# Eight stores of half-size sums from GpSimd's queue to the sync engine's, with new engine orders (one core, attention and a gated MLP)

## The chip, the cores and the metric

The kernel runs on one core of a Trainium2 chip. The metric is device time in microseconds (us). TensorE (PE) does the matmuls, VectorE (DVE) elementwise work, ScalarE (ACT) copies and activations. GpSimd (POOL) and the sync engine (SP) issue transfers here and compute next to nothing. Transfers run on 16 DMA engines, whichever engine issues them.

## The reference

Inputs are bfloat16. `x` is 2048 tokens by 1024; the MLP is 3584 wide; attention has 32 heads of 32, each token looking at 8 earlier tokens at a distance of 0, 2, ..., 14.

```python
xn = layernorm(x)
q, k, v = split(xn @ wqkv)                     # 32 heads of 32
logits = einsum("bhsd,bhswd->bhsw", q, kg) * scale     # kg: k at positions s - 2w, w = 0..7
attn = softmax(where(mask, logits, -1e9))
s = einsum("bhsw,bhswd->bhsd", attn, vg) @ wo
h = silu(xn @ w1) * (xn @ w3)
g = silu(h @ w2)
return x + s * g
```

## The kernel before

The 2048 tokens are two halves (`b` = 0, 1) of 1024, each made of two chunks of 512 (`c` = 0 to 3). For a half the order of work is: layer norm and a transposition of x, the q, k and v products, the up and gate products in 14 steps of 256 columns (`up_step`), the down product (`mlp_down`), and the output projection (`wo`). Attention runs on DVE beside these matmuls. Every matrix product is done in the Strassen-Winograd way: seven products of quarter blocks in place of eight, with sums and differences of blocks made by DVE beforehand and added up by ACT and DVE afterwards. So DVE has much to do for the matmuls too.

Many of the sums are of weights, the same for both halves of the tokens. In the first half they are stored to DRAM and in the second half they are loaded back.

`mlp_down(b)` contracts over 3584 in two halves, `fh`. It takes seven products, each 4 groups (128 tokens each, `g`) of 14 matmuls, with operands of plain down weights (`w2`, loaded in two parts `q` of 896 KB) or of sums of them (`t2`, loaded from `t_dram`). Two of the seven are split once more the same way (`product2`): these are called `l1` (plain weights) and `l2` (a sum). Each needs four half-size sums of its weights, made by DVE in the first half: `l1t1` to `l1t4`, `l2t1` to `l2t4`. Each is 448 KB, and a `dma` call stores it to `lt_dram` (`put_l10` to `put_l13` and `put_l20` to `put_l23`; the last digit is the sum's number less one). In the second half `get_l..` loads them. Beside the weights' sums there are sums of the left operand, `l1s1` to `l1s4` and `l2s1` to `l2s4`, also by DVE. The buffer of `l2t1` and of `l2s1` is the one in which x of the next chunk lay; `l2t1` therefore waits until that x is transposed into `xT` (four transposing transfers, `turn2_0` to `turn2_3`, issued by ACT, after the normalisations `nrm2_0` to `nrm2_3`). The first part of the last plain down weights is loaded into that buffer in turn; the second part into one that is free earlier. The four transpositions of the chunk after it (`turn3_0` to `turn3_3`) are issued by SP.

The order of the work is not left to a scheduler of the compiler. `Plan` records every operation with a cost, a simulation of the five engines' queues makes an order for each engine (`simulate`), and `ORDER`, five lists of moves, one for each engine, changes these orders: `(a, b)` takes operation `a` out and puts it behind `b`. Each engine runs its list in order and waits where an operand is not ready. For a transfer the cost is a size in KB times a factor by name (`COST`) over a rate (`plan.rate`). These costs only decide the order; they change no transfer.

A transfer is issued by the engine that `dma` is given:

```python
def dma(eng, name, o, a, rd, wr, kb, late=0.0):
    e = {SP: nc.sync, POOL: nc.gpsimd, ACT: nc.scalar}[eng]
```

All matmuls of plain tiles are recorded by the helper at line 582, those of the split products at 1542 (down) and 1271 (up); DVE's sums at 591, ACT's copies at 596, transfers at 623, transpositions at 784 and 792. So in the profile a line is a helper's, and an operation is told by its tile and its time. In the profile's tile names, `r` is any of the six weight buffers, `ltl_dram` is `lt_dram`, `a` holds attention's products, `E` the softmax weights, `xs` sums of x or of the left operand, `mm` the PSUM banks and `k` the buffers that hold copies of PSUM.

Of the kernel before, what the change touches and what calls it, by code (L numbers as in the profile page):

```python
# [14 lines left out]
PE, DVE, ACT, POOL, SP = range(5)  # L15
# [27 lines left out]
class Plan:  # L43
# [409 lines left out]
def kernel(  # L453
# [27 lines left out]
    NQ = 7  # L481
# [49 lines left out]
    plan = Plan()  # L531
# [891 lines left out]
    def mlp_down(b):  # L1423
# [71 lines left out]
        def product2(ps, w, bdt, xa, xc, ya, yc, sa, sc, rows, tdst, names, marks=(None, None), mixed=False):  # L1495
# [9 lines left out]
            def tsum(q, fn, x, y, rd):  # L1505
# [3 lines left out]
                if names in KEEP:  # L1509
                    dma(POOL, f"put_{names}{q}", lambda: lt_dram[names][:, q].rearrange("p (k n) -> p k n", k=NQ), T[q][0], T[q][1],  # L1510
                        [("lt", names, q)], 448)
# [575 lines left out]
```

## Time and profile before

| | us |
|---|---|
| median of 3 runs | 710.08 (709.66 to 711.32) |
| the profiled execution | 710.87 |
| its span, first to last instruction | 708.2 |
| PE busy | 699.8 |
| DVE busy | 677.0 |
| ACT busy | 386.6 |
| POOL busy | 47.1 |

The granted TensorE clock is 1.0 all through. Matmuls overlap each other in the records: one of 512 columns is listed with 379 ns, and the next begins 216 ns after it. A row of the timeline gives start, duration, engine (with q for its sequencer, which issues transfers), line, operation, tiles written and read, sizes, how many instructions it merges, and in brackets the idle time before it with what ended it. A row of the chain of waits gives start, duration and what the chain ran through. "DMA to landing" counts from the issue of a transfer to the signal that all of it has arrived.

### The profile page before, as it was taken

How to read it: one execution, taken by the hardware profiler on the slowest of the kernel's cores; microseconds unless marked ns; L12 is line 12 of the kernel's file. 1: busy time of each engine (PE TensorE's matmuls, PEld its weight loads, DVE VectorE, ACT ScalarE, POOL GpSimd, SP SyncE). 2: the span in 40 equal slices, each digit the busy share in tenths (PEclk: the TensorE clock that was granted, in tenths of full speed). 3: DMA queues.
4: the chain of work that ended last, by engine and by line, in shares of the span. 5: the costliest groups of instructions: out<-in, count | busy, mean ns of one | idle time of the engine just before them, and what ended most of it. 6: DMA issues, size and time to landing. Idle time of an engine off the chain costs nothing.

```text
span 708.2 us, 9862 instructions
## 1 busy us (share of the span) xinstructions
PE 699.8 (99%) x3666; PEld 374.5 (53%) x3666; DVE 677.0 (96%) x831; ACT 386.6 (55%) x752; POOL 47.1 (7%) x91
## 2 busy tenths in 40 slices
PE   9999999999999999899999999999999999999997
PEld 5555555555555574644555554555555555656443
DVE  7899999999999999999979999999999999999777
ACT  7654465558656795911655345566756764311053
POOL 1001010111110110100010000000100010000000
PEclk9999999999999999999999999999999999999999
DMA  9999699887968899895896577967487647977403
GB/s 329 288 339 372 204 318 322 277 260 257 337 210 268 307 289 213 248 304 156 303 289 217 178 261 222 317 203 238 147 255 226 199 155 244 306 236 240 148 32 118
DMA packets 138239, 174.06 MB, mean 246 GB/s; under 512 B 16912, under 2 KB 112800, under 8 KB 131536
## 3 DMA queue, kind: packets, MB, share of 16 engines
q1 hardware_dynamic: 126416, 134.43, 60.1%
q0 software_dynamic: 7120, 37.51, 14.6%
q10 hardware_dynamic: 4656, 1.51, 1.3%
q8 instruction: 28, 0.46, 0.3%
q14 instruction: 19, 0.16, 0.1%
HBM read 117.31 MB, written 43.78 MB: 227 GB/s over the span
## 4 chain that ended last, share of the span: by engine, by line
PE 93%; DVE 3%; DMA 2%; issue 1%; SPq 0%; DVEq 0%
PE mm L582 83%; PE mm L1271 6%; PE mm L1542 5%; DMA r<-in_B_w_dram 2%; DVE xT L591 1%; DVE h_sb L591 1%; DMA r<-in_A_x_dram 1%; DVE r L591 0%; DVE a L591 0%; PE mm L769 0%; DVE small L687 0%; DVE xs L591 0%; DVE qo L591 0%; DVE r L703 0%; SPq L623 0%
## 5 line engine op out<-in xcount | busy, mean ns | idle before, releaser
L582 PEld LDWEIGHTS <-r 128*128 128x128 f16 (+1 forms) x2068 | 219.7, 108 | 191.8 <-DMA r<-in_A_wqkv_dram 0.7
L582 PE MATMUL mm<-xs,r 128*128 128x512 f16 x1280 | 304.7, 379 | 0.0
L582 PE MATMUL mm<-xT,r 128*128 128x512 bf16 (+2 forms) x788 | 182.8, 370 | 0.1
L596 ACT COPY k<-mm 128x512 f32<-128x512 f32 (+1 forms) x226 | 120.8, 565 | 62.9 <-PE mm L582 44.8
L596 ACT COPY mm<-mm 128x512 f32<-128x512 f32 (+1 forms) x157 | 75.4, 485 | 125.5 <-PE mm L582 37.2
L582 PE MATMUL mm<-r,h_sb 128*128 128x512 f16 (+1 forms) x592 | 130.4, 379 | 2.7 <-DMA r<-in_B_w_dram 2.7
L582 PEld LDWEIGHTS <-h_sb 128*128 128x128 f16 (+1 forms) x680 | 66.5, 98 | 81.6 <-issue 3.0
L591 DVE TENSOR_TENSOR a<-a 128x2048 bf16<-128x2048 bf16 (+7 forms) x106 | 106.8, 1011 | 0.6
L591 DVE TENSOR_TENSOR h_sb<-mm,k 128x1024 bf16<-128x1024 f32 x48 | 58.2, 1218 | 5.4 <-PE mm L582 3.7
L1271 PE MATMUL mm<-xT,r 128*128 128x256 f16 (+1 forms) x364 | 61.0, 273 | 0.0
L591 DVE TENSOR_TENSOR a<-qo,kT 128x2048 bf16<-128x2048 bf16 x48 | 57.6, 1216 | 0.1
L591 DVE TENSOR_TENSOR h_sb<-h_sb 128x1024 f16<-128x1024 bf16 (+7 forms) x74 | 54.7, 749 | 0.4 <-ACT h_sb L1132 0.2
L1271 PEld LDWEIGHTS <-r 128*128 128x128 f16 (+1 forms) x364 | 35.6, 98 | 31.9
L591 DVE TENSOR_TENSOR k<-mm,k 128x1024 f32<-128x1024 f32 (+1 forms) x44 | 44.8, 1023 | 6.6 <-PE mm L582 6.6
L591 DVE TENSOR_TENSOR a<-E,vT 128x2048 bf16<-128x2048 bf16 x42 | 50.2, 1218 | 0.0
L613 ACT ACTIVATE h_sb<-mm 128x512 bf16<-128x512 f32 x60 | 36.3, 611 | 13.9 <-PE mm L582 13.6
L591 DVE TENSOR_TENSOR r<-r,r 128x1024 f16<-128x1024 f16 (+7 forms) x56 | 42.4, 768 | 0.2
L613 ACT ACTIVATE k<-k 128x512 bf16<-128x512 f32 x56 | 34.6, 635 | 12.1 <-DVE k L591 12.1
L591 DVE TENSOR_TENSOR qo<-qo,a 128x2048 bf16<-128x2048 bf16 x32 | 39.0, 1219 | 0.2
L591 DVE TENSOR_TENSOR r<-r 128x256 f16<-128x256 bf16 (+4 forms) x71 | 36.0, 514 | 0.1
L591 DVE TENSOR_TENSOR h_sb<-h_sb,k 128x2048 bf16<-128x2048 bf16 x28 | 34.1, 1218 | 1.3 <-ACT k L596 1.3
L596 ACT CAST k<-mm 128x512 bf16<-128x512 f32 x56 | 32.7, 596 | 3.0 <-PE mm L582 3.0
(131 smaller groups left out, 536.3 us busy)
## 6 DMA issues: line engine op xcount, KB each, us to landing
r<-in_B_w_dram SPq DMA_DIRECT2D x42, 512.0 KB, 5.9
s_dram<-r POOLq DMA_DIRECT2D x14, 1024.0 KB, 5.5
r<-s_dram SPq DMA_DIRECT2D x14, 1024.0 KB, 5.5
r<-t_dram SPq DMA_DIRECT2D x15, 896.0 KB, 7.4
r<-in_A_wqkv_dram SPq DMA_DIRECT2D x10, 1024.0 KB, 8.3
r<-in_B_w_dram SPq DMA_DIRECT2D x11, 896.0 KB, 6.5
h_sb<-in_B_w_dram SPq DMA_DIRECT2D x14, 512.0 KB, 8.5
t_dram<-h_sb POOLq DMA_DIRECT2D x7, 1024.0 KB, 6.2
```

Of the source, the lines that this page charges most:

```text
L582: nc.tensor.matmul(cut(ps.ap()), lhsT=lhs[k](), rhs=cut(rhs[k]()), start=(first and k == 0), stop=(last and k == n - 1), skip_group_check= ...
L591: plan.op(DVE, name, lambda: fn(out=o(), in0=a(), in1=b()), rd, wr, occ, 0.08, late=late)
L596: plan.op(ACT, name, lambda: nc.scalar.copy(out=o(), in_=a()), rd, wr, occ, 0.11)
L613: plan.op(ACT, name, lambda: nc.scalar.activation(out=o(), in_=a(), func=ACTF.Silu), rd, wr, occ, 0.11, table="silu")
L1271: nc.tensor.matmul(half(pa[i].ap, n)(), lhsT=A[0][k](), rhs=B[0][k](), start=first and k == 0, stop=k == 1, skip_group_check=True)
L1542: nc.tensor.matmul(half(bank.ap, n)(), lhsT=a[k](), rhs=c[k](), start=first and k == 0, stop=k == NQ - 1, skip_group_check=True)
```

## The change

The eight stores go out on SP's queue. The cost factors are replaced by others, with new names among them, and so is one rate; the order that the simulation makes is therefore another one, and the five lists of moves are replaced. The operations, their operands, their dependences and their sizes are the same in both kernels. The two programs have the same instructions on PE, DVE and ACT in other orders: of PE's 911 operations 357 stand at another place (at most 10 places away), of DVE's 828, 539, of ACT's 727, 542. POOL issues 70 planned transfers where it issued 78, SP 259 where it issued 251.

```diff
 ORDER = (
-    ((230, 233), (247, 237), (261, 248), (263, 249), (259, 263), ...
+    ...
-    COST = (("w1.", 1.09), ("w3.", 1.09), ("st.", 1.05), ("wqkv", 1.0), ("w2q", 1.04), ("t_dram", 0.98), ("put_sq", 0.97), ("s_dram", 0.85),
-            ("s2", 1.5), ("L", 0.74), ("E", 0.83), ("getk", 1.23), ("getv", 1.35), ("getq", 1.22), ("t2_", 1.15), ("wo", 1.12),
-            ("out", 0.98), ("movev", 1.26), ("putk", 1.1), ("putq", 1.2), ("put_l", 1.43), ("get_l", 1.1))
+    COST = (("w1.", 1.17), ("w3.", 1.17), ("st.", 1.07), ("wqkv", 0.95), ("w2", 1.08), ("t_dram", 1.07), ("put_sq", 0.95), ("s_dram", 0.97),
+            ("s2_dram", 1.05), ("s2.", 1.6), ("L", 0.72), ("E", 0.9), ("getk", 1.12), ("getv", 1.4), ("getq", 1.1), ("t2_", 1.02), ("wo", 1.06),
+            ("out", 1.2), ("movev", 1.05), ("putk", 1.15), ("putq", 1.1), ("putv", 1.05), ("put_l", 1.27), ("get_l", 1.21), ("half", 1.35),
+            ("sq", 1.2), ("xr", 1.1))
...
                 if names in KEEP:
-                    dma(POOL, f"put_{names}{q}", lambda: lt_dram[names][:, q].rearrange("p (k n) -> p k n", k=NQ), T[q][0], T[q][1],
+                    dma(SP, f"put_{names}{q}", lambda: lt_dram[names][:, q].rearrange("p (k n) -> p k n", k=NQ), T[q][0], T[q][1],
                         [("lt", names, q)], 448)
...
         else:
-            plan.rate = 3.5e5
+            plan.rate = 2.8e5
             softmax(c0 - 1)
```

Around the second of the two products the orders of SP and PE read, in the plan's names (the last plain down weights are `w2` parts 1 and 2; PE's groups are named by product and group):

```
SP before:  getv1, w2 part 1, w2 part 2, turn3_2, t2_010, turn3_3, turn3_1, t2_011, turn3_0
   after:   getv1, put_l20, w2 part 2, w2 part 1, put_l22, put_l23, put_l21, t2_010, t2_011, turn3_3, turn3_2, turn3_1, turn3_0
PE before:  l2 pair (sum 2), six l2 groups and more, w2 part 1 group 0, group 3, w2 part 2 group 3, ...
   after:   l2 pair (sum 2), one T2 group, the l2 groups, w2 part 1 group 0, group 3, group 2, w2 part 2 group 3, ...
ACT before: nrm2_3, nrm2_2, ..., nrm2_0, turn2_0, nrm2_1, turn2_1, turn2_2, Silu, turn2_3
   after:   nrm2_1, nrm2_0, ..., nrm2_3, turn2_1, turn2_0, Silu, nrm2_2, turn2_3, turn2_2
```

249 rows, old and new, of the table ORDER are left out of this document.

## The prediction

> **What bounds the kernel now.** I read the page first: its head, TensorE's and VectorE's busy shares, and the chain that ended last.
>
> ```profile
> span 708.2 us, 9862 instructions
> PE 699.8 (99%) x3666; PEld 374.5 (53%) x3666; DVE 677.0 (96%) x831; ACT 386.6 (55%) x752; POOL 47.1 (7%) x91
> PE 93%; DVE 3%; DMA 2%; issue 1%; SPq 0%; DVEq 0%
> ```
>
> TensorE (PE) is busy for all but 8.4 us and carries 93% of the chain. So the matmuls are the floor, and only their waits can be won. Next I asked for the busy time of PE in stretches, to see where those 8.4 us lie.
>
> ```profile
> 20.00:289.00 269.00, 268.96 (x1410) 1.00 0.86 282
> 289.00:302.00 13.00, 10.29 (x79) 1.00 1.05 274
> 302.00:704.00 402.00, 402.00 (x2054) 1.00 0.68 218
> ```
>
> The first column after the stretch is its length, the next PE's busy time. One stretch of 13 us loses 2.71 us, and the 671 us around it 0.04. The rest of the 8.4, 5.65, lies in the first 20 us and the last 4, where the change leaves the loads and the last stores much as they stand. The chain of waits of that stretch and the timeline say what PE waited for.
>
> ```profile
> 269.87 3.04 PE mm L582 x14
> ...
> 282.73 1.00 DVE h_sb L591
> ...
> 289.01 0.38 SPq L623
> ...
> 289.44 12.08 DMA r<-in_B_w_dram
> ...
> 284.83 1.67 PE L582 MATMUL mm<-r,h_sb 128*128 128x512 f16 x7
> 286.34 1.69 PE L1542 MATMUL mm<-r 128*128 128x256 f16 x14
> ...
> 295.65 2.92 PEld L582 LDWEIGHTS <-h_sb 128*128 128x128 f16 x15 [0.17 <-DMA r<-in_B_w_dram]
> 295.66 3.20 PE L582 MATMUL mm<-r,h_sb 128*128 128x512 bf16 x14
> 301.56 6.63 PE L582 MATMUL mm<-r,h_sb 128*128 128x512 bf16 x30 [2.71 <-DMA r<-in_B_w_dram]
> ```
>
> This is the down projection of the first half of the tokens. Two loads of plain down weights (`w2`, each 896 KB, the two halves of the contraction) leave the sync engine (SP) at 289.01 and 289.44. The first lands just as PE gets to it: the weight load at 295.65 shows 0.17 us of waiting. The second takes 12.08 us and holds PE for 2.71 us. Nothing else between 20 and 704 us holds PE, so **the most that any order can win here is 2.71 + 0.17 = 2.88 us**.
>
> Why 12.08? The stores that the change moves are in flight at that very time; they are GpSimd's rows. The DMA view has what the loads and stores took, and the windows how full the 16 DMA engines were.
>
> ```profile
> 290.24 0.95 POOL L623 DMA_DIRECT2D ltl_dram<-r  x1 [1.67 <-DVE r L591]
> 293.77 0.94 POOL L623 DMA_DIRECT2D ltl_dram<-r  x1 [2.58 <-DVE r L591]
> ltl_dram<-r POOLq DMA_DIRECT2D x4, 448.0 KB, 6.0
> DMA to landing us min/median/max: 6.6/9.3/12.1
> 295.00:298.00 3.00, 3.00 (x18) 1.53 (x17) 2.97 (x4) 3.00 (x5) 0.00 (x0) 1.00 1.05 390
> 298.00:301.50 3.50, 0.85 (x4) 0.29 (x3) 3.43 (x5) 3.48 (x5) 0.00 (x0) 1.00 1.19 202
> ```
>
> The third and fourth stores go out at 290.24 and 293.77, behind the second load but on another queue; the two loads take 6.6 and 12.1 us for the same bytes. From 295 to 301.5 the DMA engines are full (share over 1), though at 298 only 202 GB/s move. The load that PE waits for shares the engines with two stores nobody waits for at that moment.
>
> **The change part by part.** In before, each store of a half-size sum waits on GpSimd's queue, which has nothing else to do then. In after it stands in SP's queue, which issues in order: what it waits for also holds back what is behind it. The order of the two programs gives SP around the wait as: store of sum 1, second `w2`, first `w2`, stores of sums 3, 4 and 2, then the next loads (`t2`) and the four transpositions of x. So the second load leaves earlier, and three stores that raced it stand behind both.
>
> Second `w2`: its buffer is free long before. It is issued behind the first store, that is when VectorE (DVE) has made sum 1 (`l2t1`), about 284.4 by the times below. With either duration above, 6.6 or 12.1 us, it lands by 296.5; PE gets to it at 301.56 − 2.88 = 298.7, and after puts one more group of seven matmuls in front (1.51 us, the step from 284.83 to 286.34), so 300.2. **The 2.71 us go.**
>
> What is late next: the first `w2`, and DVE's sums that PE needs before it. PE's order moves that group of seven from before the first pair of sum products (286.34) to behind it; PE now comes there at 286.34 − 1.51 = 284.8. DVE's rows for what must be ready, and ScalarE's (ACT) for the transpositions that `l2t1` waits for (it overwrites the x buffer that they read):
>
> ```profile
> 280.37 1.22 DVE L591 TENSOR_TENSOR a<-a 128x2048 bf16<-128x2048 bf16 x1
> 281.50 1.22 DVE L591 TENSOR_TENSOR a<-qo,kT 128x2048 bf16<-128x2048 bf16 x1
> ...
> 283.64 1.09 DVE L591 TENSOR_TENSOR r<-r 128x1792 f16<-128x1792 f16 x1
> 284.64 0.62 DVE L591 TENSOR_TENSOR r<-xs 128x896 f16<-128x896 f16 x1
> ...
> 267.81 1.24 ACT L731 ACTIVATE r<-r,small 128x1024 bf16<-128x1024 bf16 x1 [1.41 <-issue]
> 269.08 5.64 ACTq L792 DMA_TRANSPOSE xT<-r  x2
> 274.75 1.28 ACT L613 ACT_TABLE_LOAD   x1 [5.70 <-issue]
> 274.82 1.27 ACTq L792 DMA_TRANSPOSE xT<-r  x1
> 276.05 1.09 ACT L613 ACTIVATE xs<-mm 128x512 bf16<-128x512 f32 x2
> ...
> DMA to landing us min/median/max: 3.1/6.6/9.9
> ```
>
> `l2t1` starts at 283.64, and the first product operand (`l2s1`) is ready at 285.26, 1.6 later. To be in time for 284.8, `l2t1` must start by 283.2. The issue of the first `w2` waits for a later sum of the same run: 5.4 us after `l2t1` in before (289.01), 6.4 in after, because one gate sum (1.00, the chain's row at 282.73) comes in between. With the first load's 6.6 us it lands 13.0 after `l2t1`; PE wants it at 295.66 − 0.17 = 295.5. So **`l2t1` must start by 282.5; each us later costs one**.
>
> When will it start? DVE itself: that gate sum and an attention sum (1.13, from 280.37 to 281.50) move behind it, so 283.64 − 2.1 = 281.5. The transpositions: after makes the last of the four wait for a normalisation that ACT runs behind a Silu. That Silu waits for PE's group that ends at 269.87 + 3.04 = 272.9; then a table load (1.28), the Silu (0.55, half of the pair at 276.05) and the normalisation (1.24) make 276.0, and the last transposition leaves at about 276.1. It lands 3.1, 6.6 or 9.9 us later by the four of before (least, median, most): 279.2, 282.7 or 286.0. The 9.9 belongs to one that was held in issue (5.64 us for two) because another had left 1.4 us ahead; in after the first two leave five us before the last two, but the last two leave together. I take the median, 282.7, 0.2 late, and 0.3 us for it with the issue's slack. By the bounds it costs between 0 and 3.5.
>
> First four stores (the other product, 246 to 262 us): two of them go ahead of a `w2` load.
>
> ```profile
> 260.64 21.31 PE L582 MATMUL mm<-r,h_sb 128*128 128x512 bf16 x98
> DMA to landing us min/median/max: 6.5/7.2/7.9
> 249.50 2.87 SPq L623 DMA_DIRECT2D r<-in_B_w_dram  x2
> ```
>
> That load left at 249.50 and took 6.5, so 256.0; PE comes to it at 260.64. Two stores of 448 KB ahead of it are 0.92 MB: 2.4 us at the 390 GB/s of the row from 295 to 298, 4.5 at the 202 of the row after it. The 4.6 us of cover hide either; without them it would cost that much. The stores' own waits on SP end with sums that DVE makes before these loads' buffers are free, so I cost them at nothing.
>
> The wait that this adds: the store of sum 4 holds SP until DVE has made that sum. In before the store left 10.1 us after `l2t1` began (293.77 − 283.64); I take the same, 292.8. Queued behind it are the store of sum 2, the next `t2` loads and the transpositions of x.
>
> ```profile
> 297.43 0.86 SPq L623 DMA_DIRECT2D r<-t_dram  x1
> 347.75 1.89 PE L582 MATMUL mm<-xs,r 128*128 128x512 f16 x8
> ```
>
> The first `t2` leaves at about 294.5, three us before its 297.43. The second needs the buffer that two of the stores read: with the 6.0 us of a store it leaves at about 300, and the four transpositions after it. What they feed, PE's matmuls on the differences `xs`, begins at 347.75: over 40 us of cover, so nothing.
>
> Elsewhere PE has no wait that could go, so the new orders can only lose. Most moves are by a few places inside the same step. The one I can price is in the second half's K weights: after puts three of SP's four copies of the softmax weights (`E`) ahead of the second K load.
>
> ```profile
> 364.80 1.22 SPq L623 DMA_DIRECT2D E<-a  x2
> 374.51 1.89 PE L582 MATMUL mm<-xT,r 128*128 128x512 bf16 x8
> r<-in_A_wqkv_dram SPq DMA_DIRECT2D x1, 1024.0 KB, 7.7
> DMA to landing us min/median/max: 4.9/6.4/9.7
> ```
>
> Three issues from 364.80 at 0.61 each: the load leaves at 366.6 and not before the copies. At its 7.7 us it lands at 374.3, at the copies' worst 9.7 at 376.3; PE's group that uses it comes second from 374.51, at 375.4. Between nothing and 0.9 us; I take nothing, since 7.7 is that load's own row.
>
> **The sum.** −2.88 + 0.3 = −2.6 us: a span of 705.6. The profiled run took 710.87, 2.7 over its span, and is itself 0.8 above the median of 710.08. Median after: 710.08 − 2.6 = **707.5**. 0.2%, 1.42 us, is about what a measurement of this kernel can tell from no change; the lines are 708.66 and 711.50.
>
> **The rivals.** First, the late transposition: it lands after 9.9 us, `l2t1` starts at 286.0 and PE waits 3.5 us in the sum products: −2.88 + 3.5 = +0.6, 710.7. For it: the last two leave together, as the slow pair did. Against: half of the four took 6.6 or less.
>
> Second, the other side, the wait changes its load. PE needs the first `w2` before the second, and after issues it second. If the second in line takes 12.1 us again, it leaves at 282.7 + 6.4 = 289.1 and lands at 301.2, 5.7 us after 295.5: −2.88 + 5.7 = +2.8, 712.9. It decides against the change from a landing of 298.4, 9.3 us after issue. For it: in before, second in line meant 12.1. Against: there it left 0.43 us behind the first, here 4.7 behind, and the stores follow it.
>
> Third, the change of queue does nothing: the same stores and loads go through the same full DMA engines in the same ten us, the last load lands as late, and the 2.71 us stay: 710.1. The Trainium skill's page "DMA: Bandwidth & Descriptors", section "Issuing engines are not separate DMA queues", speaks for it: transfers issued from different engines run on the same 16 DMA engines and interleave, and the choice of engine saves issue time alone. By that rule, the trace agrees that the two streams interleave (202 GB/s at share 1.19); what it does not cover is that in one queue the stores come after.
>
> Fourth, another place becomes late: 671 us without a wait hold many just-in-time hand-overs, and every engine's order changes there. Bounds: nothing, or a wait as large as the one the present order left, 2.7. In the middle, 707.5 + 1.4 = 708.9, up to 710.2.
>
> **How the numbers follow.** Forecast 0.52; late transposition 0.16, of which 0.04 beyond 711.5; the other load 0.14, of which 0.12 there; queue does nothing 0.07; another place 0.11, of which 0.03 still under 708.66 and 0.06 as a sum with the other losses beyond 711.5. Faster 0.52 + 0.03 = 0.55; slower 0.04 + 0.12 + 0.06 = 0.22; same 0.23. The range begins where all 2.88 go and the median of three falls 0.4 low, 706.8, and reaches over the late transposition and the queue that does nothing to 711.5; the slower 0.22, less what lies just at its edge, is what it leaves out. The likeliest case's own range is 706.9 to 708.6.
>
> **What would show it.** Right: PE without an idle over 0.5 us between 285 and 302; the second `w2` issued ahead of the first, both landing before PE wants them; the stores' rows on SP. Late transposition: the sum products wait for DVE, and `l2t1` starts right after a landing of `xT`. Other load: a wait at the first of those matmuls with DMA as releaser. Wrong altogether: a PE wait of over 1 us in another stretch, first of all around the K weights near 372.

## The result and the profile after

The changed kernel takes 707.19 us, median of 10 runs (706.91 to 709.21); the kernel before, run beside it, 710.00, median of 10 (708.89 to 712.96). The ratio is 0.9959, with a 95% interval of 0.9946 to 0.9973: faster by 0.41%, 2.8 us. The forecast was 707.5. The first lines of the page after, its windows, and all that PE waited for. The lists of moves are longer, so a helper's line is 11 or 12 higher than before: 593 for 582, 602 for 591, 634 for 623; in the experiments it differs again.

```profile
span 705.4 us, 9790 instructions
PE 696.8 (99%) x3611; PEld 374.5 (53%) x3666; DVE 676.4 (96%) x831; ACT 385.4 (55%) x752; POOL 40.6 (6%) x83
PE 94%; DVE 3%; DMA 2%; issue 1%; SPq 0%; ACT 0%; DVEq 0%; ACTq 0%
```

```profile
20.00:289.00 269.00, 267.84 (x1390) 144.89 (x1410) 262.78 (x339) 171.37 (x334) 24.72 (x46) 1.00 0.86 285
289.00:302.00 13.00, 12.95 (x90) 8.70 (x90) 12.72 (x19) 11.38 (x16) 0.00 (x0) 1.00 1.03 309
302.00:701.00 399.00, 397.17 (x2007) 208.69 (x2037) 383.51 (x429) 189.02 (x374) 13.00 (x24) 1.00 0.68 216
```

```profile
PE mm L575 <- DVE k L573: 1.3, 1, 1.3
PE mm L781 <- DVE r L715: 0.3, 1, 0.3
PE mm L593 <- DMA r<-s_dram: 0.2, 1, 0.2
```

The rows of the second fence give a stretch, its length, the busy time of PE, PE's weight loads, DVE, ACT and GpSimd, the granted clock, the DMA share and GB/s. The last fence lists the engine and line, what it waited for, the sum in us, how many times and the longest. The 2.7 us behind `in_B_w` are no longer there; what is left lies in the first 20 us and, for the last 0.2, at 452. PE's busy time seems to have fallen by 3 us, but that is the record: 3611 matmuls are listed where the weight loads are 3666, so 55 records are missing, one every 12 us or so; each shows as some 0.05 us that are not busy (1.16 us in the first window, 1.83 in the third, where 0.2 is all that waits). The end of PE's work is the better measure. The last row of PE's timeline, before and after:

```profile
703.26 1.04 PE L607 MATMUL mm<-h_sb,qo 128*128 128x256 f16 x8
```

```profile
700.38 1.04 PE L618 MATMUL mm<-h_sb,qo 128*128 128x256 f16 x8
```

It is 2.88 us earlier, the whole of what the prediction called the most that any order can win; the span went from 708.24 to 705.36, by the same 2.88. In the stretch itself, PE's timeline, SP's, and the loads' times from issue to landing:

```profile
284.60 1.69 PE L1554 MATMUL mm<-r 128*128 128x256 f16 x14
286.13 1.67 PE L593 MATMUL mm<-r,h_sb 128*128 128x512 f16 x7
...
295.28 7.93 PE L593 MATMUL mm<-r,h_sb 128*128 128x512 bf16 x35
```

```profile
282.89 0.34 SPq L634 DMA_DIRECT2D ltl_dram<-r  x1
283.32 5.19 SPq L634 DMA_DIRECT2D r<-in_B_w_dram  x2
289.11 4.28 SPq L634 DMA_DIRECT2D ltl_dram<-r  x3
293.44 4.76 SPq L634 DMA_DIRECT2D r<-t_dram  x2
298.30 6.85 SPq L804 DMA_TRANSPOSE xT<-r  x3
```

```profile
L634 SPq DMA_DIRECT2D r<-in_B_w_dram x2: 372/379/386, 283.3 to 288.1; - x2
...
DMA to landing us min/median/max: 5.5/5.7/5.8
```

PE runs from 284.60 into the plain matmuls at 295.28 and on through 35 of them with no bracket, that is, no wait. SP has the order that was forecast: store of sum 1 (282.89), the second `w2` (283.3), the first (288.1), three stores, two `t2`, the transpositions. The two `w2` loads took 5.8 and 5.5 us where the second part had taken 12.1 and the first 6.6, and landed at 289.2 and 293.7; PE came to the first of these at 299.8 (21 matmuls of 216 ns behind 295.28) and to the second at 295.28.

### The profile page after: what moved, and what is told of

It reads as the page before. It is cut to its first block, busy times and chain, and to the rows that moved or that the text cites. A ratio compares the mean times of both kernels' runs of the same rounds, so it can differ in the third digit from the quotient of the medians.

```text
span 705.4 us, 9790 instructions
## 1 busy us (share of the span) xinstructions
PE 696.8 (99%) x3611; PEld 374.5 (53%) x3666; DVE 676.4 (96%) x831; ACT 385.4 (55%) x752; POOL 40.6 (6%) x83
## 3 DMA queue, kind: packets, MB, share of 16 engines
q10 hardware_dynamic: 4656, 1.51, 1.0%
## 4 chain that ended last, share of the span: by engine, by line
PE 94%; DVE 3%; DMA 2%; issue 1%; SPq 0%; ACT 0%; DVEq 0%; ACTq 0%
PE mm L593 82%; PE mm L1554 6%; PE mm L1283 5%; DMA r<-s_dram 1%; DVE r L602 1%; DVE a L602 1%; DMA r<-in_A_x_dram 1%; DMA out_dram<-r 1%; PE mm L781 0%; DVE small L699 0%; SPq L634 0%; DVE r L715 0%; DVE xT L602 0%; DVE E L602 0%; ACT k L607 0%
## 5 line engine op out<-in xcount | busy, mean ns | idle before, releaser
L593 PEld LDWEIGHTS <-r 128*128 128x128 f16 (+1 forms) x2068 | 219.6, 108 | 192.0 <-DMA r<-in_A_wqkv_dram 0.5
L593 PE MATMUL mm<-xT,r 128*128 128x512 bf16 (+2 forms) x747 | 177.6, 369 | 2.1
L1283 PEld LDWEIGHTS <-r 128*128 128x128 bf16 (+1 forms) x364 | 35.6, 98 | 32.0
L602 DVE TENSOR_TENSOR r<-r 128x1024 f16<-128x1024 bf16 (+4 forms) x71 | 36.1, 515 | 0.2
```

Of the source, the lines that this page charges most:

```text
L593: nc.tensor.matmul(cut(ps.ap()), lhsT=lhs[k](), rhs=cut(rhs[k]()), start=(first and k == 0), stop=(last and k == n - 1), skip_group_check= ...
L602: plan.op(DVE, name, lambda: fn(out=o(), in0=a(), in1=b()), rd, wr, occ, 0.08, late=late)
L1283: nc.tensor.matmul(half(pa[i].ap, n)(), lhsT=A[0][k](), rhs=B[0][k](), start=first and k == 0, stop=k == 1, skip_group_check=True)
```

## The experiments

The prediction was right in number. What had to be tested is whether for its reason: that two stores on another queue stretched the second `w2` load. **Theory 1** says so. **Rival 2** came from looking at SP's rows of before again. Behind the second load, at 293.77, SP issues a transposition of x (`turn3_2`), which the prediction had passed over; it is in flight until after the load has landed, and the changed orders move it away together with the stores. So the transposition may have stretched the load. In the last 3.5 us of that load most packets are under 512 B, which those of loads and stores are not: 22 of 959 between 295 and 299 in `b_turn_later` below, which has no transposition then. The DMA view of before, 298 to 301.5:

```profile
DMA packets 1001, 0.71 MB, mean 202 GB/s; under 512 B 823, under 2 KB 896, under 8 KB 1001
```

**Theory 3** is that the order of the two loads does it all, whatever shares the engines. All kernels keep the operations and move some in the engines' rows after the planner and the lists of moves have made them: `(e, i, b)` takes operation `i` out of its row and puts it behind `b` on engine `e`.

```diff
-        self.order = self.timed(self.listed())
+        rows = self.listed()
+        for e, i, b in MOVES:
+            for row in rows:
+                if i in row:
+                    row.remove(i)
+            rows[e].insert(rows[e].index(b) + 1, i)
+            self.ops[i].eng = e
+        self.order = self.timed(rows)
...
-        plan.op(eng, name, lambda: e.dma_start(out=o(), in_=a()), ...
+        n = len(plan.ops)
+        plan.op(eng, name, lambda: {SP: nc.sync, POOL: nc.gpsimd, ACT: nc.scalar}[plan.ops[n].eng].dma_start(out=o(), in_=a()), ...
```

The operations: `w2` first part 1354, second 1355; stores `put_l10` to `put_l13` 1213, 1223, 1216, 1241; `put_l20` to `put_l23` 1306, 1318, 1310, 1335; `turn3_0` to `turn3_3` 1346 to 1349; `t2` 1372, 1373; load of v 1476. A ratio is against runs of before taken beside the run's own; their median lay between 709.88 and 710.74, so ratios are compared and not medians.

**What stretches the load: four corners.** The stores of sums 3 and 4 are beside the second load or not, and so is the transposition; before, with all of them, is the first corner. Then the stores alone are put on SP, in before's orders.

```diff
+MOVES = ((SP, 1213, 1193), (SP, 1216, 1213), (SP, 1223, 1269), (SP, 1241, 1223), (SP, 1306, 1476), (SP, 1318, 1355), (SP, 1310, 1318), (SP, 1335, 1310),)
```

> The kernel before with one thing changed: the eight stores stand in SP's queue (sums 1 and 3 of the first product ahead of that product's loads of w2, the others behind them; sum 1 of the second ahead of the two late w2 loads, sums 2, 3 and 4 behind them and ahead of the transposition turn3_2). All engine orders else are before's; the first w2 load still goes ahead of the second. Theory 1, the prediction's (the stores on another queue stretched the second w2 load from 6.6 to 12.1 us): with them behind it in one queue it takes about 7 us, lands by 297, and PE's wait at 301.6 falls from 2.71 us to 0.2 or less; median 707.3 to 707.6. Rival 2 (what stretches that load is the transposition of x that SP issues at 293.77 behind it, whose packets are small): turn3_2 still leaves at about 294, the load lands at 299 to 301.5, and PE waits 0.5 to 2.7 us; median 707.9 to 710.1.

Measured: 707.47 us (6 runs), ratio 0.996 [0.9946, 0.9974]. How long the two loads took, and PE's one new wait:

```profile
DMA to landing us min/median/max: 5.4/6.5/7.6
```

```profile
PE mm L591 <- DVE h_sb L600: 0.7, 1, 0.7
```

The second load took 7.6 us and PE did not wait for it: the move of the queue alone takes that wait away. It does not yet tell theory 1 from rival 2, since the stores in front held the transposition back to 296.37. And a new wait shows: 0.7 us at 416, PE for a DVE sum. DVE, which runs in order, had lost 2.3 us at 370 waiting for a copy of the softmax weights `E` (0.9 in before), and in before PE came there later. This is the prediction's fourth rival, in before's orders; the changed ones do not have it.

Next the transpositions alone are moved, with the stores left on GpSimd.

```diff
+MOVES = ((SP, 1349, 1373), (SP, 1347, 1349), (SP, 1348, 1347),)
```

> The kernel before with one thing changed: on SP the four transpositions of the last x (turn3_2, turn3_3, turn3_1, turn3_0) stand behind both loads of t2 instead of between and ahead of them; the stores stay on GpSimd at their times. Theory 1 (the stores stretch the second w2 load): nothing changes for it, 12 us, PE waits 2.7 us; median 710. Rival 2 (the transposition at 293.77 stretches it): it lands by 297 to 298.5 and PE's wait falls to 0.2 or less; median 707.3 to 707.6. If both share the blame the wait lies between, 0.5 to 1.5 us.

Measured: 709.29 us (12 runs), ratio 0.9975 [0.9964, 0.9986]. How long the loads took, and PE's timeline:

```profile
DMA to landing us min/median/max: 6.6/8.7/10.9
...
300.31 2.97 PE L591 MATMUL mm<-r,h_sb 128*128 128x512 bf16 x13 [1.51 <-DMA r<-in_B_w_dram]
```

The load still takes 10.9 us and PE still waits 1.51, at the upper edge of the case in which both share the blame. The fourth corner leaves the transposition beside the load and takes the two stores away, behind it.

```diff
+MOVES = ((SP, 1310, 1348), (SP, 1335, 1310),)
```

> The kernel before with one thing changed: the stores of sums 3 and 4 of the second product stand in SP's queue behind turn3_2, so that the transposition is beside the second w2 load and these two stores are not (the fourth corner: both beside it gave a landing at 301.5, stores alone 300.3, neither 296.8). Theory 1 (the two stores stretch the load): it takes 7 to 8 us, lands by 297.5, PE waits 0.3 us or less; median 707.4 to 707.7. Rival 2 (the transposition stretches it): lands at 299 to 301, PE waits 0.7 to 2.5 us; median 708.2 to 710.

```profile
DMA to landing us min/median/max: 6.3/7.4/8.5
```

Measured: 706.93 us (7 runs), ratio 0.9948 [0.9927, 0.9968]; the load takes 8.5 us, half a microsecond more than theory 1 had at most; PE has no wait over 0.1 us after the first 20. Moving these two stores behind the load is worth as much as the whole change: the intervals of the two overlap, so neither beats the other.

Each of the two stores alone was the next question.

```diff
+MOVES = ((SP, 1310, 1348),)      # b_s3_behind_turn
+MOVES = ((SP, 1335, 1348),)      # b_s4_behind_turn
```

> The kernel before with one thing changed: the store of sum 3 alone (it leaves GpSimd at 290.24, 0.8 us behind the second w2 load) stands in SP's queue behind turn3_2; the store of sum 4 stays on GpSimd. With both behind turn3_2 the load took 8.5 us instead of 12.1. If each store adds its share of bytes (half of 3.6 us), the load lands at about 299.5 and PE waits 0.6 to 1.1 us; median 707.9 to 708.4. If the store that leaves first does the harm, it lands by 297.9 and PE waits 0.3 us or less; median 707.0 to 707.4. If the other does, nothing changes: 709.5 to 710.5.

> The kernel before with one thing changed: the store of sum 4 alone (it leaves GpSimd at 293.77, 4.3 us behind the second w2 load) stands in SP's queue behind turn3_2; the store of sum 3 stays on GpSimd. If each store adds its share of bytes, the load lands at about 299.5 and PE waits 0.6 to 1.1 us; median 707.9 to 708.4. If the store that leaves first does the harm, nothing changes: 709.5 to 710.5. If this one does, it lands by 297.9 and PE waits 0.3 us or less; median 707.0 to 707.4.

Measured: 707.67 (10 runs), ratio 0.9967 [0.9954, 0.9979], and 707.70 (10 runs), 0.9972 [0.9958, 0.9987]. The load took 8.3 and 9.8 us; in the second case PE waits 0.4:

```profile
DMA to landing us min/median/max: 6.2/7.3/8.3
```

```profile
DMA to landing us min/median/max: 6.6/8.2/9.8
...
299.03 4.26 PE L591 MATMUL mm<-r,h_sb 128*128 128x512 bf16 x19 [0.40 <-DMA r<-in_B_w_dram]
```

Neither came out as one of the three cases throughout. Without the store of sum 3 the load and the wait are those of the second case (the store that leaves first does the harm), but without the store of sum 4 not all of the harm stays. Taking either store away is nearly enough, so the shares do not add: 3.7 and 2.3 us singly, 3.6 together.

| in flight beside the second `w2` | its time | PE waits for it |
|---|---|---|
| both stores and the transposition (before) | 12.1 | 2.71 |
| both stores (`b_turn_later`) | 10.9 | 1.51 |
| store of sum 3, transposition (`b_s4_behind_turn`) | 9.8 | 0.40 |
| store of sum 4, transposition (`b_s3_behind_turn`) | 8.3 | none |
| transposition (`b_s34_behind_turn`) | 8.5 | none |
| neither (`b_stores_sp`) | 7.6 | none |

The stores account for 3.3 (10.9 against 7.6) to 3.6 us (12.1 against 8.5), the transposition for 0.9 to 1.2. Each is one execution, and where the same things were in flight as in before, the load once took 11.3 (the run `b_pe_group` below): 0.8 is scatter. The stores' share is far beyond that, so theory 1 holds for the larger part; rival 2 holds for about a quarter at most, and its share is hardly beyond the scatter. That share may be smaller still, since two corners differ in more. In `b_stores_sp` the store of sum 2 is on SP's queue too, behind the loads; in the other rows it is on GpSimd's, and in before it is nearly all that moves between 289 and 291 (0.46 MB, and 0.01 of SP's queue). In `b_turn_later` the first `t2` load leaves at 290.50, right behind the second `w2`, and not at 297.43. The clean pair is before against `b_s34_behind_turn`, 12.1 against 8.5: it differs in the two stores. The DMA view of 295 to 299, by queue (packets, MB, share of the 16 engines; q0 is GpSimd's, q1 SP's), before and with the stores on SP:

```profile
q0 software_dynamic: 203, 0.77, 59.3%
q1 hardware_dynamic: 827, 0.75, 57.5%
```

```profile
q1 hardware_dynamic: 2394, 1.41, 112.3%
```

With two queues the stores move 0.77 MB while SP's queue, with the load in it, moves 0.75: an even split in these 4 us, whoever is in a hurry. It begins late: from 291 to 295 GpSimd's queue moves nothing, although the store of sum 3 left at 290.24; why is left open. In one queue all 1.41 MB are SP's, and load and stores land in the order of their issue: the load at 296.8, the stores at 298.1, 299.4 and 302.0.

**The order of the loads.** In before, only the second `w2` is put ahead of the first; and in the changed kernel that is undone.

```diff
+MOVES = ((SP, 1354, 1355),)      # b_w2_swapped
+MOVES = ((SP, 1355, 1354),)      # a_w2_swapped
```

> The kernel before with one thing changed: on SP the second w2 load stands ahead of the first; stores on GpSimd, transpositions and all other orders as before. Its buffer is free long before, so it leaves right behind the load of v (about 280.2) and lands by 290. The first w2 load then is the last in line: it leaves at 289.0 as before. Theory 3 (the earlier issue is what counts, whatever shares the engines later): the first load takes 6 to 7 us, lands at 295 to 296, PE waits 0 to 0.5 us; median 707.2 to 707.8. Theories 1 and 2 in their strong form (the last load in line is stretched to 12 us by stores or by the transposition): it lands at 301, and PE, which wants it at 295.5, waits 5.6 us; median 713.

> The changed kernel with one thing undone: on SP the first w2 load stands ahead of the second again, both ahead of the stores of sums 3, 4 and 2. The pair then leaves at 288.1 and 288.5. Theory 1 (in one queue the stores come after): the first lands at 294, the second at 296 to 297, PE, which wants them at 295.5 and 300.2, does not wait; median 707.1 to 707.4, so the swap is not needed. Theory 3 (only the earlier second load helps): the second lands after 300.2 and PE waits 0.5 us or more; 707.7 or more.

Measured: 707.08 (6 runs), ratio 0.9956 [0.994, 0.9972], and 707.65 (10 runs), 0.9963 [0.9951, 0.9975]. In the first, the second `w2` leaves at 280.16 and lands at 288.0; the other, now last in line, lands 5.7 us after its issue, at 294.9, although the store of sum 3 leaves 0.7 us behind it. PE does not wait. In the second, the pair lands at 294.6 and 297.4, and PE does not wait for it either. Its profiled execution, the slowest of the ten (708.92), lost 1.2 us more than after's in the first 20 us, where the loads of `wqkv` were late; whether its median is above the expectation for the same reason is not shown. So either half of the change is enough: the queue without the order, or the order without the queue. The strong form of theories 1 and 2, that whichever load is last in line gets stretched, fell. A load that does not queue behind another one of 896 KB is nearly through before the stores get in its way: between 291 and 293 SP's queue moves 0.54 MB in the first of these runs and GpSimd's nothing.

**The changed orders with the stores back on GpSimd.**

```diff
+MOVES = ((POOL, 1213, 957), (POOL, 1216, 1213), (POOL, 1223, 1216), (POOL, 1241, 1223), (POOL, 1306, 1241), (POOL, 1318, 1306), (POOL, 1310, 1318), (POOL, 1335, 1310),)
```

> The changed kernel with one thing undone: the eight stores are GpSimd's again, in the order that they had before; all engine orders else are the changed kernel's. Theory 1 (stores on another queue stretch the load that they race): the first w2 load, last in line, leaves at about 288.1, shares the engines with the stores of sums 3 and 4 and takes 9 to 12 us, lands at 297 to 300, PE waits 1.6 to 4.7 us; median 708.8 to 711.9. Rival 2 (the transpositions did it, and they now stand behind the loads) and theory 3 (the earlier second load does it): no PE wait over 0.3 us; median 707.2 to 707.5.

```profile
296.43 6.86 PE L602 MATMUL mm<-r,h_sb 128*128 128x512 bf16 x30 [0.36 <-DMA r<-in_B_w_dram]
```

Measured: 707.74 us (6 runs), ratio 0.9961 [0.9947, 0.9975]. The first `w2` leaves at 289.88, not 288.14, because the store of sum 1, whose buffer it takes, landed only at 289.75 from GpSimd's queue (from SP's at 286.39). It takes 6.5 us, and PE waits 0.36 us. Theory 1 had this load at 9 to 12 us, too much. So within the changed orders the queue is worth little more than this wait.

**One more group of matmuls ahead, in before.**

```diff
+MOVES = ((PE, 1364, 1368),)
```

> The kernel before with one thing changed: PE's order takes one more group of seven matmuls, whose operands have landed, ahead of the first one that needs the second w2 load (as in the changed kernel). The prediction gave this 1.51 us. If the load lands at 301.5 as before, PE's wait falls from 2.71 to 1.2 us; median 708.6. If the profiled execution's late landing was not usual, the median falls by less.

Measured: 708.15 us (12 runs), ratio 0.9961 [0.9947, 0.9974]; PE's wait falls to 0.22. The group hides its 1.51 us, as said; the load, 11.3 us in this execution, was 0.8 shorter by itself.

**The prices of the rivals.** A late transposition (the last normalisation, operation 1190, and the last two transpositions, 1284 and 1280, later on ACT), first by a little, then by more:

```diff
+MOVES = ((ACT, 1190, 1281), (ACT, 1284, 1190), (ACT, 1280, 1284),)      # a_turn2_late
+MOVES = ((ACT, 1190, 1199), (ACT, 1284, 1190), (ACT, 1280, 1284),)      # a_turn2_later
```

> The changed kernel with one thing changed: on ACT the last normalisation of x and the last two transpositions stand one Silu later, which tests the prediction's first rival (a late transposition). In the changed kernel the last one left at 274.45, landed at 282.59, and the left-operand sum that writes behind it (l2s1) began at 282.79, PE taking it at 284.60. With it 2.5 to 4 us later, that sum starts at 285 to 286.6; if the chain of the prediction holds, PE waits 1.8 to 3.4 us in the sum products; median 709.0 to 710.6. If there is slack that the prediction did not see: no wait over 0.5 us, 707.2 to 707.7.

> The changed kernel with one thing changed: on ACT the last normalisation of x and the last two transpositions stand behind the next Silu, the halo copy and a mean, some 3 us later than in the changed kernel (the shift before this one was 0.66 us only and showed nothing). The last transposition then leaves at 276.5 to 278.5 and lands at 284 to 286.5 instead of 282.6. If the prediction's chain holds from the left-operand sum on (ready by 284.6), PE waits 0.9 to 3.4 us in the sum products, and the first w2 load leaves as much later; median 708.1 to 710.6. If there is slack that the prediction did not see: no wait over 0.5 us, 707.2 to 707.7.

The first came out at 707.24 us (9 runs), ratio 0.995 [0.9932, 0.9969]. It settles nothing: the transposition left at 275.11, only 0.66 us later, and landed at 282.86. The second took 711.10 (10 runs), ratio 1.0016 [1.0005, 1.0028], all of the gain lost and more. DVE's row and PE's, and windows (the columns behind the busy times are the granted clock, the DMA share and GB/s):

```profile
282.02 1.09 DVE L611 TENSOR_TENSOR r<-r 128x1792 f16<-128x1792 f16 x1
286.38 0.62 DVE L611 TENSOR_TENSOR r<-xs 128x896 f16<-128x896 f16 x1 [3.28 <-DMA xT<-r]
```

```profile
287.07 2.40 PE L1565 MATMUL mm<-r 128*128 128x256 f16 x14 [2.08 <-DVE r L611]
289.26 2.70 PE L602 MATMUL mm<-r,h_sb 128*128 128x512 f16 x7
```

```profile
288.00:289.00 1.00, 1.00 (x7) 0.74 (x5) 1.00 (x3) 0.96 (x3) 0.00 (x0) 0.50 1.09 348
289.00:291.00 2.00, 2.00 (x8) 0.80 (x6) 2.00 (x4) 1.22 (x4) 0.00 (x0) 0.50 0.15 46
291.50:293.00 1.50, 1.50 (x15) 1.17 (x13) 1.50 (x3) 0.00 (x0) 0.00 (x0) 1.00 0.00 0
```

The transposition landed at 286.26, and the left-operand sum behind it began at 286.38, 3.28 us idle. PE waited 2.08 us, and then ran at half clock until 291.3: 14 matmuls of 256 columns took 2.40 us, not 1.69, and seven of 512 took 2.70, not 1.67. That is another 1.7 us, and the span grew by 4.0, to 709.4; so the time is 0.5 us above the upper end of the expectation, whose wait of 0.9 to 3.4 us held.

The last one puts the stores of sums 3 and 4 ahead of the first `w2` in SP's queue.

```diff
+MOVES = ((SP, 1310, 1355), (SP, 1335, 1310),)
```

> The changed kernel with one thing changed: in SP's queue the stores of sums 3 and 4 stand ahead of the first w2 load instead of behind it. The store of sum 4 waits for VectorE until 292.4, and the load behind it in the queue with it. Theory 1 with an in-order queue: the load leaves at 292.8 instead of 288.14, takes 5.5 to 6.5 us, lands at 298.3 to 299.3, and PE, which wants it at 295.5, waits 2.8 to 3.8 us; median 710.0 to 711.0: the gain of the change is gone, by the place in the queue alone. If loads take the engines ahead of a waiting store in the same queue: no wait, 707.2.

```profile
299.81 3.50 PE L602 MATMUL mm<-r,h_sb 128*128 128x512 bf16 x8 [4.32 <-DMA r<-in_B_w_dram]
```

```profile
301.00:303.00 2.00, 2.00 (x6) 0.73 (x5) 1.97 (x3) 1.29 (x2) 0.00 (x0) 0.50 1.07 366
304.00:306.00 2.00, 2.00 (x11) 0.88 (x9) 1.97 (x2) 0.00 (x0) 0.00 (x0) 1.00 1.68 316
```

Measured: 713.93 us (12 runs), ratio 1.0044 [1.003, 1.0059]: with the same queue and another place in it, the kernel is 3.3 us slower than before (710.58 in these runs). The load left at 292.99, behind the store that waits for DVE, and landed at 299.76. PE waited 4.32 us, more than the 2.8 to 3.8 expected, and again lost 1.7 us to the half clock, which no expectation had.

## Why the prediction was right, and where it was not

**The bound and the sum.** PE's only real wait went, and nothing took its place: −2.88 us, the prediction's bound. The forecast had −2.6, span 705.6 and median 707.5; the measured are 705.36 and 707.19. The mis-sized term is the 0.3 for the late transposition: it was 0.

**The cause.** The stores were named, and are shown to be the larger part by the four corners. The transposition that SP issued at 293.77 was missing from the argument; it adds at most about 1.2 us to the 12.1. The rival "the queue does nothing" is refuted by the queue alone (707.47). But the prediction gave the gain to two things at once, the earlier second load and the stores behind both, and did not see that each is enough by itself: in before's orders 707.08 for the earlier load alone and 706.93 for the two stores behind it alone. In the changed kernel the new queue adds little to the new orders, which take 707.74 without it. The Trainium skill's page "DMA: Bandwidth & Descriptors", section "Issuing engines are not separate DMA queues", says that transfers from different engines run on the same 16 DMA engines and interleave, and that issuing from several saves issue time alone. The trace agrees with the first half (0.77 and 0.75 MB in the same 4 us). The second does not follow for one transfer among them: the same load takes 12.1 us with the two stores interleaved and 8.5 with them behind it.

**Second `w2`.** Forecast to leave at 284.4 and land by 296.5, it left at 283.32 and landed at 289.17: right, and 10 us before PE came for it.

**What is late next.** `l2t1` began at 281.78, by DVE alone, where 281.5 was forecast. But the step that made it wait for the last transposition, which stands in the description of the kernel as well, was wrong. That one landed at 282.59, after `l2t1` had begun, and in the run with the later transposition `l2t1` kept its time (282.02) while `l2s1` waited. `l2s1` is the sum that waits, one sum later. And `l2s1` is made in two parts: the 285.26 at which the prediction had it ready in before is the end of the first, and the second, which begins at 285.18, ends 0.5 us later. ACT's rows and how long the four transpositions took in the changed kernel:

```profile
268.86 1.28 ACT L624 ACT_TABLE_LOAD   x1
272.69 0.60 ACT L624 ACTIVATE xs<-mm 128x512 bf16<-128x512 f32 x1 [2.55 <-PE mm L593]
...
274.45 3.52 ACTq L804 DMA_TRANSPOSE xT<-r  x1
```

```profile
DMA to landing us min/median/max: 3.2/7.1/8.1
```

The table load that the prediction put behind PE's group ran at 268.86, ahead of it; so the transposition left at 274.45 and not 276.1, and it took 8.1 us and not 6.6. The two errors cancel, and 282.6 for 282.7 is in part luck. `l2s1` began at 282.79, 0.2 us behind that landing, and was done at 283.94; PE came for it at 284.60. So 0.7 us of slack were left, and this is the next thing to become late.

**First `w2`.** Forecast at `l2t1` plus 6.4, it left at 288.14 (281.78 + 6.36) and landed 5.5 us later: in time by 1.6 us. The rival that it would be stretched to 12.1 did not come. The first reason given against it held: the load ahead of it was nearly through (it landed 1.0 us after this one left). The second, that the stores follow it, was not needed: with the stores on GpSimd it took 6.5 us.

**The rivals' prices.** For a landing at 286.0 the prediction had a wait of 3.5 us and 710.7; forced to 286.26, the wait is 2.1 and the kernel takes 711.1. The wait was put too high, since it was counted from the wrong sum, and the loss of the clock was missing. Both errors again nearly cancel.

**The rest.** The first product's `w2` left at 249.27 behind two stores and landed before PE's 260.4. The store of sum 4 left at 292.41 (292.8 forecast), the first `t2` at 293.4 (294.5), the transpositions from 298.3 (after 300). The second K load left at 363.50 and landed at 371.5, ahead of PE's 373.84, earlier than either end of the estimate. None of these cost anything.

## What to carry to other kernels

When a load holds the bottleneck, look at all that is in flight beside it, on every queue: a transfer nobody waits for took an even share of the DMA engines from one that somebody did (0.77 against 0.75 MB in 4 us). Putting it behind the load in the same queue cured that, and so did issuing the load some microseconds earlier; either alone gave the gain here, to within 0.6 us. In a queue that runs in order the place is what counts: the same stores on the same queue, one place ahead of the load, made the kernel slower than before.

## What the runs showed of the hardware that was not expected

A wait of PE can cost more than its length. After idle stretches of 2.08 and of 4.32 us the granted clock was 0.5 for 3.4 us (287.9 to 291.3 and 299.9 to 303.4), which cost 1.7 us each; after before's 2.71 us it stayed at 1.00. The traces suggest why. Between two changes of the clock that lie inside a run there are always whole multiples of 3.413 us: before has full clock from 6.09 to 709.24, 206 times 3.413, and the two half clocks are one such length each. (Ahead of 6.09 the matmuls of 512 columns follow each other every 427 ns and not every 216, so that before's clock is 1.0 all through does not hold for its first 6 us.) So the clock seems to be set window by window. PE's busy time in these windows, with clock, DMA share and GB/s behind it, in before, then with the later transposition (`a_turn2_later`), then with the stores ahead (`a_store4_ahead`):

```profile
296.23:299.64 3.41, 2.62 (x13) 1.00 1.16 342
299.64:303.05 3.41, 1.49 (x7) 1.00 1.11 203
303.05:306.47 3.42, 3.42 (x17) 1.00 1.44 266
```

```profile
284.50:287.91 3.41, 1.32 (x11) 1.00 1.13 350
287.91:291.33 3.42, 3.42 (x13) 0.50 0.44 139
```

```profile
296.53:299.95 3.42, 0.14 (x1) 1.00 0.90 274
299.95:303.36 3.41, 3.41 (x9) 0.50 1.08 363
```

A window's edge cuts before's 2.71 us into 0.79 and 1.92; the 2.08 us all lie in one window, and 3.28 of the 4.32 do. So the limit here lies between 1.92 and 2.08 us of idle time in one window, an estimate from these three runs. The Trainium skill's page "TensorE: Matmul & The Clock Gate", section "Part 1: The HAM clock gate", puts the half clock behind an idle window of about 3.4 us that runs freely. The window's length agrees, and that the same idle time need not have the same effect; that all of the window must be idle does not, since 2.08 of 3.41 us sufficed.
